# A parallel retention layer and a snake MLP on one core: two waits of the matrix engine's queue given other neighbours

## The chip, the cores and the metric

The kernel runs on one NeuronCore of a Trainium2 chip. A core has five engines with instruction queues of their own, each in program order: TensorE (PE, matrix products into PSUM), VectorE (DVE), ScalarE (ACT), GpSimd (POOL) and SyncE (SP, which here only issues transfers). They meet through semaphores. Data move between HBM and the on-chip memory SBUF by DMA, issued from SP's, POOL's or ACT's queue. The metric is the device time of one execution in microseconds (us); lower is better.

## The reference

Eight batches of 576 tokens with 8 heads of 64 go through a retention layer (attention without softmax, with a decay per head), and its output through a two-layer MLP:

```python
scores = scale * q @ k.T                    # per batch and head
ret = scores * Dmat                         # gamma[h] ** (i - j) for j <= i, else 0
x = (ret @ v) laid out as [4608, 512]       # tokens x (heads * 64)
h = x @ w_in                                # 512 -> 2048
g = h + sin(alpha * h) ** 2 / (alpha + 1e-9)
out = g @ w_out                             # 2048 -> 512, float32
```

## The kernel before, in words

**Attention.** The first 512 tokens of a batch are four chunks of 128, taken as two halves `p` of 256. q and k come in as float32 (`raw`, six buffers) by SP's queue and are cast to float16 with the decay factors (`cast_half`, L215 on VectorE or GpSimd, L210 on ScalarE). v, w_in and w_out come by GpSimd's queue. kT and qT are made by PE transposes into PSUM (`transposes`, L275) and a copy out (`take`, L236 and L237), or, for the second half of batch 2 and for all later batches, by DMA transposes (`crossed`, L232). `scores_pe` (L376) makes the products of kT and qT in two calls `y` per half; `scores_out` (L386) casts a result to SBUF on ScalarE as `scf`; `scores_mask` (L393) multiplies by the causal mask on VectorE into `ret`, from `scf` or straight from PSUM. `outer` (L312) makes k'v of a half or of both, `first_sum`, `faded`, `next_sum`, `to_state` and `chain` (L319 to L359) carry the states along; `values` (L462) and `states` (L488) add up the output, and `take_x` (L236, L237) writes it to `x`. The 64 last tokens of all batches are gathered into an eighth extra block.

**The MLP.** Block `n` is the 512 tokens of batch `n`. Its first product is made in 16 units of four matmuls (`gemm1_pe`, L584, into one of three PSUM banks "hp"), each followed by a sine (L593) and a square (L602) on ScalarE and a product on VectorE (L609) into `gT`. The second product of a block comes in 16 parts, four for each output chunk `c` of 128 tokens, each of four matmuls (`gemm2_pe`, L623); part `g` needs group `g` of w_out. A chunk adds up in one bank ("op", of which there is one, or "hp"), is copied to `osb` and written out.

**PSUM.** Eight banks: two double banks "mm" (transposes, scores, k'v, attention output take turns), three "hp", one "op".

**What sets the order.** The program is recorded in the written order, and each engine runs its own instructions in that order. Up to the start of block 2, the order is a table (`TABLE`, L637 on) of one step per line, read by `follow` (L1146). Its words here: `G2 n c g bank` four products of the second MLP layer; `SP`, `SO`, `SM` scores, their cast out, their mask (batch, half, y); `C b nm p t e` the cast of half of one tile on engine V, A or G; `WO g` the load of w_out's group g on GpSimd's queue; `TR` and `TK` PE transposes and their copies out; `OU` outer products. From block 2 on (L1160), a loop over the 16 units of block `n` puts, in each unit: the first product and its sine, then the steps that `at_unit` has set for this unit, then four products of the second layer of the block before (`next_second`) with the square and product around them. In block 2 the set steps are the attention of batch 3 (L1169 to L1172). The same loop casts batch 4 on GpSimd in units 5 to 9 (`CASTS`, L1159), issues its DMA transposes in units 7 and 10, and loads batch 5 from unit 12 on. The `chain` of batch 3 comes ahead of these casts on GpSimd.

Two parts of the second layer of block 1 are made inside the table, so in block 2 an output chunk closes in units 1, 5, 9 and 13, and there the order is: products, chunk copy (L633), square, product.

Of the kernel before, what the change touches and what calls it, by code (L numbers as in the profile page):

```python
# [16 lines left out]
def kernel(  # L17
# [103 lines left out]
    def load_v(b, p):  # L121
        t_ = work.tile([P, H, 2, D], F16, tag="v16", bufs=6, name="v16")
        half[b, "v", p] = t_
        if split(b):
            for g, s, xs in pieces(b, p):
                nc.gpsimd.dma_start(t_[halves(g), :, s], v[b, :, xs, :].rearrange("h i d -> i h d"))  # L126
            return None
        i_ = nc.gpsimd.dma_start(
            t_.rearrange("p h r d -> p h (r d)"),
            v[b, :, 256 * p : 256 * p + 256, :].rearrange("h (i r) d -> i h (r d)", r=2),  # L130
        )
        half[b, "v", p] = t_
        return i_

    def load_rest_v(G):
        t_ = work.tile([P, 2 * H, D], F16, tag="vr16", bufs=1, name="v16")
        for e in range(2):
            b = 4 * G + 2 * e
            nc.gpsimd.dma_start(t_[halves(e)], v[b : b + 2, :, 512:576, :].rearrange("b h i d -> i (b h) d"))
        half[G, "v", "rest"] = t_  # L140

    def load(b, nm, p):
        t_ = work.tile([P, H, 2 * D], F32, tag="raw", bufs=6, name=nm + "32")
        raw[b, nm, p] = t_
        if split(b) and nm == "k":
            for g, s, xs in pieces(b, p):
                nc.sync.dma_start(
                    t_[halves(g), :, 64 * s : 64 * s + 64], src[nm][b, :, xs, :].rearrange("h i d -> i h d")
                )
            return None  # L150
        return nc.sync.dma_start(t_, src[nm][b, :, 256 * p : 256 * p + 256, :].rearrange("h (i r) d -> i h (r d)", r=2))
# [13 lines left out]
    def load_rest(G, nm):  # L165
        t_ = work.tile([P, H, 2 * D], F32, tag="raw", bufs=6, name=nm + "32")
        for e in range(2):
            b = 4 * G + 2 * e
            nc.sync.dma_start(
                t_[halves(e)].rearrange("p h (x d) -> p (h x) d", d=D),  # L170
                src[nm][b : b + 2, :, 512:576, :].rearrange("b h i d -> i (b h) d"),
            )
        raw[G, nm, "rest"] = t_
# [29 lines left out]
    def cast_half(b, nm, p, t, eng):  # L203
        if (b, nm, p) not in half:
            half[b, nm, p] = work.tile([P, 4, 2, 2, D], F16, tag=nm + "16", bufs=nbuf[nm], name=nm + "16")
        if eng is nc.scalar:
            for y in range(4):
                for r in range(2):
                    h = head_of(y, t)
                    eng.mul(  # L210
                        half[b, nm, p][:, y, r, t, :], raw[b, nm, p][:, h, D * r : D * r + D],
                        fac[nm][:, 2 * h + r : 2 * h + r + 1],
                    )
            return
        eng.tensor_tensor(  # L215
            half[b, nm, p][:, :, :, t, :],
            raw[b, nm, p].rearrange("p (a t) (r d) -> p a t r d", t=2, r=2)[:, :, t],
            (ct if nm == "k" and split(b) else fac[nm]).rearrange("p (a t r) -> p a t r", a=4, t=2)[:, :, t].unsqueeze(3).to_broadcast([P, 4, 2, D]),
            MULT,
        )  # L220
# [354 lines left out]
    def gemm1(n, fc, o=None):  # L575
        gemm1_pe(n, fc, o)
        sine(n, fc)
# [20 lines left out]
    def square(n, fc, eng):  # L598
        hps, s_t = hps_of[n, fc]
        ss_t = work.tile([P, 512], F16, tag="ss", bufs=4, name="ss_t")  # L600
        if eng is nc.scalar:
            nc.scalar.activation(ss_t, s_t, mybir.ActivationFunctionType.Square)  # L602
        else:
            eng.tensor_tensor(ss_t, s_t, s_t, MULT)  # L604
        hps_of[n, fc] = hps, ss_t

    def product(n, fc):
        hps, ss_t = hps_of.pop((n, fc))
        nc.vector.scalar_tensor_tensor(gT[n][:, fc, :], ss_t, inva[:, fc : fc + 1], hps, MULT, ADD)  # L609
# [187 lines left out]
LK 2 q 1 w_in1  # L797
C 1 k 1 1 V
TK 1 0 q V
G2 0 3 1 hp  # L800
SP 1 0 1
SP 1 0 0
SO 1 0 1
C 1 k 1 0 V
SO 1 0 0
SM 1 0 0
C 1 q 1 1 G
WO 3
C 1 q 1 0 G
TR 1 1 q  # L810
TR 1 1 k
TK 1 1 q V
G2 0 2 1 hp
TK 1 1 k A
SP 1 1 0
# [169 lines left out]
    with tc.manual_schedule():  # L985
# [34 lines left out]
        def of(b):  # L1020
            if b not in att:
                att[b] = Attention(b)
            return att[b]
# [77 lines left out]
        def next_second(k=0):  # L1101
            n, u = second.pop(0)
            gemm2(n, u, "hp" if n == NBLK - 1 and u > 3 else "op")
# [56 lines left out]
        for n in range(2, NBLK):  # L1160
            A = A2
            todo = {}

            def at_unit(u, *fs):
                todo.setdefault(u, []).extend(fs)

            if A:
                if n == 2:
                    at_unit(1, lambda: A.scores(0, 0), lambda: A.scores(0, 1))  # L1169
                    at_unit(4, lambda: A.outer((0, 1)), lambda: A.chain((0, 1, 2, 3)), lambda: A.scores(1, 0))  # L1170
                    at_unit(7, lambda: A.scores(1, 1), lambda: A.values(0), lambda: A.add_states(0))
                    at_unit(10, lambda: A.values(1), lambda: A.add_states(1))  # L1172
                else:
                    at_unit(0, lambda: A.near(0), lambda: A.masked(0))
                    at_unit(0, lambda: A.outer((0, 1)), lambda: A.chain((0, 1, 2, 3)))
                    at_unit(4, lambda: A.near(1), A.late, lambda: A.masked(1))
                    at_unit(5, lambda: A.masked("late"))
                    if n == 5:
                        at_unit(8, lambda: A.all_values(0), rest[0].scores, lambda: A.add_states(0))
                        at_unit(11, lambda: A.all_values(1), rest[0].values, lambda: A.states(1, last=True))  # L1180
                        at_unit(11, lambda: A.take_x(1, V))
                    else:
                        at_unit(8, lambda: A.all_values(0), lambda: A.all_values(1))
                        at_unit(8, lambda: A.states(0, last=True), lambda: A.states(1, last=True))
                        at_unit(8, lambda: A.take_x(0, A_), lambda: A.take_x(1, V))
            bn = n + 2
            if bn < B:
                A2 = of(bn)
                at_unit(0, lambda: load_v(bn, 0), lambda: load_v(bn, 1))
                for i, u in enumerate(CASTS[n]):  # L1190
                    p, nm, t = i // 4, "kq"[i // 2 % 2], i % 2
                    at_unit(u, lambda p=p, nm=nm, t=t: cast_half(bn, nm, p, t, V if n > 2 else G_))
                at_unit(CASTS[n][3] + 1, lambda: A2.crossed(0))
                at_unit(CASTS[n][7] + 1, lambda: A2.crossed(1))
            else:
                A2 = None
            if bn + 1 < B:
                for i, (p, nm) in enumerate(HALVES):
                    at_unit(i + 12, lambda nm=nm, p=p: load(bn + 1, nm, p))
            if n in (3, 5):  # L1200
                at_unit(15, *[lambda nm=nm: load_rest((n - 3) // 2, nm) for nm in "kq"])
                at_unit(15, lambda: load_rest_v((n - 3) // 2))
            R = rest[(n - 4) // 2] if n in (4, 6) else None
            if n in (4, 6):
                at_unit(11 if n == 4 else 5, lambda: cast((n - 4) // 2, "k", "rest", V))
                at_unit(13 if n == 4 else 8, lambda: cast((n - 4) // 2, "q", "rest", V), lambda: R.crossed())
            if n == 7:
                at_unit(0, lambda: rest[1].scores())
                at_unit(2, lambda: rest[1].values())
            for u in range(16):  # L1210
                gemm1(n, u)
                for f in todo.get(u, []):
                    f()
                last = second[0][1] % 4 == 3
                if not last:
                    square(n, u, A_)
                    product(n, u)
                next_second()
                if last:
                    square(n, u, A_)  # L1220
                    product(n, u)
# [44 lines left out]
```

## Time and profile before

| | us |
|---|---|
| runs, median of 3 (lowest to highest) | 310.55 (310.01 to 310.61) |
| profiled execution | 309.65 |
| its span, first to last instruction | 307.6 |
| PE busy in the span | 296.1 |
| ScalarE busy | 227.0 |
| VectorE busy | 192.5 |
| GpSimd busy | 134.3 |

The profile is of one execution, and its times count from the span's first instruction. Matmuls are pipelined, so neighbouring ones overlap in the record; lengths of groups are therefore read from start to start. A timeline row gives start, length, engine, line, operation, output and inputs, the count, and in square brackets the idle time just before and what ended it. The views that the text names are the busy time by stretches, the waits by engine, the timelines by engine, the chain of work that ended last, and the transfers with their time from issue to landing. In the table's stretch (to about 77 us) the engines take turns in setting the pace; block 2 begins at 77.2 us.

### The profile page before, as it was taken

What the parts mean: (1) busy time and instruction counts of PE and PEld (TensorE: products, weight loads), DVE (VectorE), ACT (ScalarE), POOL (GpSimd) and SP (SyncE); (2) the same over time, 40 slices, a digit from 0 to 9 for tenths busy, and PEclk for the clock granted to TensorE, in tenths of its full rate; (3) what the DMA queues carried; (4) which work ended last, traced back from release to release, by engine and by line L of the source; (5) the groups of instructions that cost most, each with busy time, mean ns of one, the idle gap of its engine ahead of it and who ended that gap; (6) DMA issues with size and microseconds to landing.
All of it is one profiled execution on the core that took longest, in us unless ns stands there. A gap on an engine that the chain in (4) does not pass through costs nothing.

```text
span 307.6 us, 7628 instructions
## 1 busy us (share of the span) xinstructions
PE 296.1 (96%) x3134; PEld 152.6 (50%) x3134; DVE 192.5 (63%) x266; ACT 227.0 (74%) x378; POOL 134.3 (44%) x158
## 2 busy tenths in 40 slices
PE   7799989999899999999999999999999999999994
PEld 7475445544445444544454445544544444444444
DVE  3879848799554357956997699546665343444301
ACT  1579864899588887788778878787877888888810
POOL 3886744869969629702970297209000000000000
PEclk9999999999999999999999999999999999999998
DMA  8999999997999896999899979985331111122133
GB/s 216 220 206 230 238 195 279 191 248 119 165 187 216 170 212 139 145 174 228 177 156 189 186 189 187 152 127 87 70 68 37 35 34 36 34 54 49 35 68 68
DMA packets 118018, 44.74 MB, mean 145 GB/s; under 512 B 84433, under 2 KB 113505, under 8 KB 117985
## 3 DMA queue, kind: packets, MB, share of 16 engines
q1 hardware_dynamic: 83792, 35.08, 57.0%
q0 software_dynamic: 33600, 8.92, 31.1%
q8 instruction: 24, 0.39, 0.6%
q10 hardware_dynamic: 592, 0.28, 0.4%
q14 instruction: 10, 0.07, 0.1%
HBM read 36.91 MB, written 9.44 MB: 151 GB/s over the span
## 4 chain that ended last, share of the span: by engine, by line
PE 81%; DVE 10%; DMA 4%; POOL 1%; ACT 1%; issue 1%; SPq 0%; DVEq 0%; POOLq 0%
PE ops L623 37%; PE hps L584 32%; DVE ret L393 4%; DVE gT L609 2%; DMA qT<-q 2%; PE o L462 2%; PE o L488 2%; DMA q<-in_q_dram 2%; PE kv L312 1%; PE tr L275 1%; PE ops L1228 1%; PE sc L376 1%; PE sc L407 1%; PE hps L1067 1%; DVE kvs L334 1%
## 5 line engine op out<-in xcount | busy, mean ns | idle before, releaser
L609 DVE SCALAR_TENSOR_TENSOR gT<-ss_t,inva,hps 128x512 f16<-128x512 f16 x136 | 100.5, 744 | 79.9 <-ACT ss_t L602 79.4
L623 PE MATMUL ops<-w_out,gT 128*128 128x512 f16 x560 | 140.8, 379 | 0.0
L584 PE MATMUL hps<-x,w_in 128*128 128x512 f16 x480 | 120.9, 379 | 1.1 <-DVE gT L609 0.9
L593 ACT ACTIVATE s_t<-hps,alpha_t 128x512 f16<-128x512 f32 x136 | 92.8, 685 | 33.3 <-PE hps L584 32.3
L584 PEld LDWEIGHTS <-w_in 128*128 128x128 f16 x544 | 53.0, 98 | 64.5 <-issue 1.5
L623 PEld LDWEIGHTS <-gT 128*128 128x128 f16 x560 | 53.0, 98 | 60.9 <-DVE gT L609 0.3
L602 ACT ACTIVATE ss_t<-s_t 128x512 f16<-128x512 f16 x127 | 79.9, 631 | 2.6
L346 POOL TENSOR_TENSOR s<-kvs,cn 128x512 f16<-128x512 f32 x28 | 30.6, 1092 | 58.4 <-ACT kvs L319 50.5
L633 ACT COPY osb<-ops 128x512 f32<-128x512 f32 x31 | 18.1, 585 | 13.5 <-PE ops L623 13.3
L126 POOL DMA_DIRECT2D v<-in_v_dram x32 | 22.0, 730 | 0.0
L393 DVE TENSOR_TENSOR ret<-sc,mask 128x1024 f16<-128x1024 f32 x12 | 14.4, 1214 | 5.7 <-PE sc L376 5.7
L215 DVE TENSOR_TENSOR q<-q,cn 128x512 f16<-128x512 f32 x17 | 15.2, 920 | 3.9 <-DMA q<-in_q_dram 3.8
L584 PE MATMUL hps<-x_rest,w_in 128*128 128x512 f16 x64 | 16.4, 379 | 0.0
L215 POOL TENSOR_TENSOR q<-q,cn 128x512 f16<-128x512 f32 x14 | 14.8, 1069 | 0.4 <-DMA q<-in_q_dram 0.4
L432 DVE TENSOR_TENSOR ret<-sc,two 128x1024 f16<-128x1024 f32 x12 | 14.6, 1217 | 0.0
L236 ACT CAST x<-o 128x1024 f16<-128x1024 f32 (+1 forms) x13 | 10.8, 851 | 4.0 <-PE o L488 3.4
L604 POOL TENSOR_TENSOR ss_t<-s_t 128x512 f16<-128x512 f16 x10 | 10.4, 1057 | 6.3 <-ACT s_t L593 3.7
L359 POOL TENSOR_TENSOR kvs<-s,kvs 128x256 f32<-128x256 f32 x15 | 11.5, 769 | 1.2
L358 POOL TENSOR_TENSOR s<-kvs,cn 128x256 f32<-128x256 f32 x15 | 10.9, 730 | 0.0
L462 PE MATMUL o<-ret,v 64*64 64x128 f16 (+1 forms) x512 | 9.7, 213 | 1.1 <-DVE ret L393 1.0
L462 PEld LDWEIGHTS <-v 64*64 64x64 f16 x512 | 7.5, 107 | 5.6 <-issue 4.2
L215 POOL TENSOR_TENSOR k<-k,cn 128x512 f16<-128x512 f32 x9 | 9.9, 1115 | 0.0
(74 smaller groups left out, 210.7 us busy)
## 6 DMA issues: line engine op xcount, KB each, us to landing
out_dram<-osb SPq DMA_DIRECT2D x70, 128.0 KB, 2.9
q<-in_q_dram SPq DMA_DIRECT2D x14, 512.0 KB, 7.1
k<-in_k_dram SPq DMA_DIRECT2D x32, 128.0 KB, 4.6
k<-in_k_dram SPq DMA_DIRECT2D x7, 512.0 KB, 7.4
q<-in_q_dram SPq DMA_DIRECT2D x8, 256.0 KB, 5.1
v<-in_v_dram POOLq DMA_DIRECT2D x8, 256.0 KB, 5.7
w_in<-in_moe_w_in_dram POOLq DMA_DIRECT2D x4, 512.0 KB, 7.5
w_out<-in_moe_w_out_dram POOLq DMA_DIRECT2D x4, 512.0 KB, 7.9
```

Source lines behind the costliest of these rows:

```text
L126: nc.gpsimd.dma_start(t_[halves(g), :, s], v[b, :, xs, :].rearrange("h i d -> i h d"))
L215: eng.tensor_tensor(half[b, nm, p][:, :, :, t, :], raw[b, nm, p].rearrange("p (a t) (r d) -> p a t r d", t=2, r=2)[:, :, t], (ct if nm == ...
L346: (eng or nc.gpsimd).tensor_tensor(d_, self.kvs[:, n].unsqueeze(2).to_broadcast([P, 4, 2, D]), g2.unsqueeze(3).to_broadcast([P, 4, 2, D]), ...
L393: nc.vector.tensor_tensor(ret.rearrange("p t (z x) -> p (t z) x", z=2)[:, :, 0:n], sc.rearrange("p t (z x) -> p (t z) x", z=2)[:, :, 0:n], ...
L432: nc.vector.tensor_tensor(ret.rearrange("p t (a x) -> p (t a) x", a=n), sc.rearrange("p t (a x) -> p (t a) x", a=n), m_.unsqueeze(1).to_br ...
L462: nc.tensor.matmul(o[g][halves(t), x0 : x0 + 128].rearrange("p (r i) -> p r i", r=2)[:, :, i0:], x, y, start=(t, g) not in begun, stop=las ...
L584: nc.tensor.matmul(hps, w_in16[:, a, fc * P : (fc + 1) * P], x_of[n][:, a], start=(a == 0), stop=(a == KT - 1),)
L593: nc.scalar.activation(s_t, hps, mybir.ActivationFunctionType.Sin, bias=0.0, scale=alpha_t[:, fc : fc + 1],)
L602: nc.scalar.activation(ss_t, s_t, mybir.ActivationFunctionType.Square)
L609: nc.vector.scalar_tensor_tensor(gT[n][:, fc, :], ss_t, inva[:, fc : fc + 1], hps, MULT, ADD)
L623: nc.tensor.matmul(ops[n, c], gT[n][:, fk, c * P : (c + 1) * P], w_out16[:, fk, :], start=(fk == 0), stop=(fk == FC - 1),)
L633: nc.scalar.copy(osb, ops.pop((n, c)))
```

## The change

Two places. In the table, for batch 1: the four products `G2 0 3 1` go from ahead of the first half's scores to behind them; the mask `SM 1 0 0` goes from ahead of the second half's transposes to behind the copy of their qT; the load `WO 3` goes from between GpSimd's two casts of q to behind both. In block 2, each of the four groups of set steps for batch 3 comes one unit later. Nothing is added or taken out.

```diff
 TK 1 0 q V
-G2 0 3 1 hp
 SP 1 0 1
 SP 1 0 0
+G2 0 3 1 hp
 SO 1 0 1
 C 1 k 1 0 V
 SO 1 0 0
-SM 1 0 0
 C 1 q 1 1 G
+C 1 q 1 0 G
 WO 3
-C 1 q 1 0 G
 TR 1 1 q
 TR 1 1 k
 TK 1 1 q V
+SM 1 0 0
 G2 0 2 1 hp
 TK 1 1 k A
 SP 1 1 0
```

```diff
                 if n == 2:
-                    at_unit(1, lambda: A.scores(0, 0), lambda: A.scores(0, 1))
-                    at_unit(4, lambda: A.outer((0, 1)), lambda: A.chain((0, 1, 2, 3)), lambda: A.scores(1, 0))
-                    at_unit(7, lambda: A.scores(1, 1), lambda: A.values(0), lambda: A.add_states(0))
-                    at_unit(10, lambda: A.values(1), lambda: A.add_states(1))
+                    at_unit(2, lambda: A.scores(0, 0), lambda: A.scores(0, 1))
+                    at_unit(5, lambda: A.outer((0, 1)), lambda: A.chain((0, 1, 2, 3)), lambda: A.scores(1, 0))
+                    at_unit(8, lambda: A.scores(1, 1), lambda: A.values(0), lambda: A.add_states(0))
+                    at_unit(11, lambda: A.values(1), lambda: A.add_states(1))
```

## The prediction

> **What bounds the kernel now.** The row of busy time by stretches comes first: before and after 81.3 us, the end of the last wait that the matrix engine has.
>
> ```profile
> 81.30:291.00 209.70, 209.70 (x2042) 101.31 (x2032) 129.31 (x164) 166.91 (x263) 76.01 (x93) 1.00 0.84 127
> 28.00:81.30 53.30, 50.02 (x655) 25.73 (x653) 41.77 (x64) 40.85 (x78) 38.18 (x41) 1.00 1.12 211
> ```
>
> Columns: stretch, length, then busy time of PE, its weight loads, DVE, ACT, POOL, the granted clock, DMA. From 81.3 to 291 PE is busy 209.70 of 209.70 us at clock 1.00: whatever moves its work earlier there moves the end, and whatever makes it wait is paid in full. From 28 to 81.3 it idles 53.30 - 50.02 = 3.28 us. The waits of PE, the view read next, name three of these where the change is: 0.9 us for ACT's scf, 0.3 for VectorE's qT, 0.8 for qT from a DMA; the rows below carry each in brackets. Then the timelines of PE, ACT, DVE and POOL around 40 us (start, length):
>
> ```profile
> 38.02 1.89 PE L623 MATMUL ops<-w_out,gT 128*128 128x512 f16 x8
> 39.84 0.64 PE L376 MATMUL sc<-qT,kT 64*64 64x128 f16 x32
> 41.37 0.61 PE L275 MATMUL tr<-ident,q 128*128 128x128 f16 x8 [0.89 <-ACT scf L386]
> 41.81 0.61 PE L275 MATMUL tr<-ident,k 128*128 128x128 f16 x8
> 43.61 0.42 PE L376 MATMUL sc<-qT,kT 64*64 64x128 f16 x16 [0.33 <-DVE qT L237]
> ...
> 38.22 1.01 ACT L236 COPY kT<-tr 128x1024 f16<-128x1024 f16 x1 [0.32 <-PE tr L275]
> 40.30 1.93 ACT L386 CAST scf<-sc 128x1024 f16<-128x1024 f32 x2 [1.08 <-PE sc L376]
> 42.46 1.01 ACT L236 COPY kT<-tr 128x1024 f16<-128x1024 f16 x1 [0.23 <-PE tr L275]
> ...
> 38.86 0.93 DVE L215 TENSOR_TENSOR k<-k,cn 128x512 f16<-128x512 f32 x1
> 42.26 0.69 DVE L393 TENSOR_TENSOR ret<-scf,mask 128x1024 f16<-128x1024 f16 x1 [2.48 <-ACT scf L386]
> 42.87 0.68 DVE L237 COPY qT<-tr 128x1024 f16<-128x1024 f16 x1
> ...
> 37.92 1.31 POOL L215 TENSOR_TENSOR q<-q,cn 128x512 f16<-128x512 f32 x1
> 39.19 0.81 POOL L107 DMA_DIRECT2D w_out<-in_moe_w_out_dram  x1
> 40.02 1.06 POOL L215 TENSOR_TENSOR q<-q,cn 128x512 f16<-128x512 f32 x1
> ```
>
> Here ACT is the link: its score casts start only when the scores do, and those stand behind eight products. The transposes at 41.37 wait for the first cast and start 1.07 after it does (40.30); GpSimd's second cast of q, behind the issue of w_out's load, ends at 40.02 + 1.06 = 41.08, in time. VectorE's mask at 42.26, waiting for the second cast, holds up the copy of qT that the next scores need.
>
> **The front, step by step.** A hand-over costs about 0.05 us (qT's copy ends at 42.87 + 0.68 = 43.55, the scores start at 43.61). Four products take 0.86: eight matmuls of this size lie between 89.33 and 91.06 in the rows of block 2, 1.73 us (half the distance from 38.02 to the scores would be 0.91; I take the steady figure).
> - Four of the eight products go behind the scores. The first four then end their issue at 38.02 + 0.86 = 38.88, and the scores wait for kT: 38.22 + 1.01 + 0.05 = 39.28 instead of 39.84. So PE idles 0.40 there, and gains 0.56.
> - ACT's casts start 0.46 after the scores (40.30 - 39.84): 39.74; with the 1.07 and the 1.93 of the row, the transposes may start at 40.81 and both casts are done by 41.67. PE does its scores (0.64) and the four moved products (0.86) by 40.78. So the transposes start at 40.81, not 41.37: the products now fill the former wait, and the casts still set it.
> - GpSimd's second cast, ahead of w_out's issue, starts about 39.19 and takes between 1.06 (alone) and 1.31 (the row beside VectorE's work): it ends by 40.25 to 40.50. Neither end binds against 40.81; I take 1.31, since VectorE's 38.86 row overlaps it.
> - The Trainium skill, SBUF — State Buffer, "Who interferes with whom", speaks against this move: a VectorE instruction with two SBUF inputs and a GpSimd one that reads SBUF exclude each other, the first holding the port to its end. By that rule the cast would start after VectorE's 38.86 + 0.93 = 39.79 and end near 40.85, the transposes would start near 40.90, and the front would gain 0.56 instead of 0.65, an estimate of 309.15 us for the whole. The rows of 1.31 and 0.93 beside each other fit it; they do not prove it.
> - kT's copy starts 0.65 after the transposes of k begin (42.46 - 41.81). Those begin at 40.81 + 0.44 = 41.25, so the copy runs 41.90 to 42.91; ACT is free from 41.67. qT's copy no longer stands behind the mask: the transposes of q end at 40.81 + 0.61 = 41.42, the copy by about 42.15. The mask then runs in VectorE's free time, and its reader is far off (the value products at 47.8 in the row below).
> - The next scores start at 42.96 instead of 43.61, now held by kT instead of qT. **Gain of the front: 0.65 us**, with about 0.4 us of idle PE before the first scores and 0.4 before the next (42.96 less 41.25 + 0.44 + 0.86, when the transposes of k and the four products after them are issued) left over.
>
> Does 0.65 last? What could stay at its old clock time are transfers:
>
> ```profile
> w_out<-in_moe_w_out_dram POOLq DMA_DIRECT2D x1, 512.0 KB, 8.8
> 37.02 0.89 POOL L128 DMA_DIRECT2D v<-in_v_dram  x1
> DMA packets 568, 0.15 MB, mean 183 GB/s; under 512 B 566, under 2 KB 568, under 8 KB 568
> ...
> DMA packets 196, 0.20 MB, mean 201 GB/s; under 512 B 0, under 2 KB 196, under 8 KB 196
> ...
> 42.91 0.86 SPq L151 DMA_DIRECT2D k<-in_k_dram  x1
> k<-in_k_dram SPq DMA_DIRECT2D x1, 512.0 KB, 8.4
> ...
> 47.79 0.45 PE L462 MATMUL o<-ret,v 64*64 64x128 f16 x16
> 48.85 3.63 PE L623 MATMUL ops<-w_out,gT 128*128 128x512 f16 x16
> 52.41 0.95 PE L462 MATMUL o<-ret,v 64*64 64x128 f16 x32
> 52.81 1.28 DVE L215 TENSOR_TENSOR k<-k,cn 128x512 f16<-128x512 f32 x2
> ```
>
> The first two rows are the last load of w_out (39.19 + 8.8 = 47.99) and the v load issued on the same queue before it. The two packet rows are of 42.0 to 42.8 and 43.5 to 44.5: first small packets alone, then large ones alone. So GpSimd's queue is at the v load's packets until about 42.5, and w_out's, issued at 39.19, stand behind them. An issue about 1.06 to 1.3 later, at 40.25 to 40.50, still comes before that, so I take a landing unchanged at 47.99; the other end is 1.06 later, 49.05. The products that need it are the sixteen at 48.85, now 48.20: covered by 0.21. Keys of batch 2 land at 42.91 + 8.4 = 51.31, and VectorE wants them at 52.81 - 0.65 = 52.16: covered by 0.85.
>
> **Block 2.**
>
> ```profile
> 78.94 1.03 PE L584 MATMUL hps<-x,w_in 128*128 128x512 f16 x4
> 80.80 0.64 PE L376 MATMUL sc<-qT,kT 64*64 64x128 f16 x32 [0.84 <-DMA qT<-q]
> ...
> 73.97 1.80 SPq L232 DMA_TRANSPOSE qT<-q  x1
> qT<-q SPq DMA_TRANSPOSE x1, 6.7
> ```
>
> The transpose of qT lands at 73.97 + 6.7 = 80.67, PE is free 0.84 earlier. One unit later the scores come after unit 1's four products and unit 2's four matmuls: 78.94 + 3 x 0.86 = 81.52 without the front's gain, 80.87 with it. The landing, moved with the front, is 80.02; unmoved, 80.67. Either way it is there first. **Gain: 0.84 us**, whole, because PE had no other wait behind it.
>
> What the later slots meet (lengths and distances inside a unit are those of before):
>
> ```profile
> 86.66 0.71 PE L312 MATMUL kv<-v,k 64*64 64x64 f16 x64
> 87.59 1.04 PE L623 MATMUL ops<-w_out,gT 128*128 128x512 f16 x4
> 89.33 1.03 PE L623 MATMUL ops<-w_out,gT 128*128 128x512 f16 x4
> 91.06 1.03 PE L623 MATMUL ops<-w_out,gT 128*128 128x512 f16 x4
> ...
> 87.49 1.01 ACT L319 COPY kvs<-kv 128x1024 f32<-128x1024 f32 x1
> 90.39 0.58 ACT L633 COPY osb<-ops 128x512 f32<-128x512 f32 x1 [0.17 <-PE ops L623]
> ```
>
> Unit 5 closes an output chunk, so the copy of kv (1.01) now stands ahead of that chunk's copy (0.58) on ACT, and the single bank of the chunk must be empty when unit 6's products start. Counted from the outer products: kv's copy runs 0.83 to 1.84; the closing products start at 0.93, their copy 1.06 later (90.39 - 89.33), at 1.99 to 2.57; the bank is wanted 1.73 after 0.93, at 2.66. So it costs nothing, by 0.09; the other end is 0.92 (the 1.01 less this margin).
>
> The outer products themselves come at 86.66 + 1.73 - 1.49 = 86.90, 0.24 later by the clock, and GpSimd's chain and its casts of batch 4 with them:
>
> ```profile
> 101.15 1.37 SPq L232 DMA_TRANSPOSE qT<-q  x1
> qT<-q SPq DMA_TRANSPOSE x1, 3.2
> q<-in_q_dram SPq DMA_DIRECT2D x1, 512.0 KB, 10.3
> 110.67 0.42 PE L407 MATMUL sc<-qT,kT 64*64 64x128 f16 x16
> ```
>
> qT of batch 4 is issued at 101.39 and, at 3.2, lands at 104.6; block 3's first scores ask for it at 110.67 - 1.49 = 109.18. Covered by 4.6 us. The moved masks and copies of x keep three units or more to their readers, and a mask that stands ahead of a unit's product on VectorE did so in the unit before; these I cost at nothing, the distances inside a unit being the same.
>
> **The sum:** 0.65 + 0.84 = 1.49 us. The profiled execution took 309.65 us, its span 307.6 (2.05 around it); it becomes 308.16. The median of the runs is 310.55, 0.90 above the profiled one, so I forecast 310.55 - 1.49 = **309.06**.
>
> **Rivals.**
> 1. *The front's gain is given back to w_out's load.* If its landing moves with its issue, to 49.05, the sixteen products start at 49.09, 0.24 later than before, and the value products at 52.65. Before, the second half of those waited until about 52.9 for a mask, so about 0.1 to nothing of the 0.65 is left: 309.62 to 309.71. For: the cover is 0.21 only. Against: the packets' order.
> 2. *The copy of kv delays the chunk's copy in unit 5.* Up to 0.92 us lost: 309.06 + 0.92 = 309.98. For: a margin of 0.09. Against: both copies' times follow PE, which spaces them.
> 3. *The change doesn't do what it says:* both waits come back at full size at the next instruction: 310.55. For the front, kT could take over from qT entirely; against, kT's own chain starts at ACT's casts, which do move.
> 4. *Slower: the late transposes of batch 4.* GpSimd's chain leaves 109.18 - 101.39 = 7.79 us for qT. The trace has 3.2 here, 6.7 at 73.97, and 10.3 for the slowest load above. At 10.3 it lands at 111.69, PE waits 2.51, and the run ends 1.02 later than before, 311.6. It is slower from a landing time of 7.79 + 1.49 = 9.3 us on. For: transfers are the least steady thing in this trace. Against: more than twice its measured time.
>
> **Chances.** Forecast 0.60; rival 1 0.15; rival 2 0.07; rival 3 0.07; rival 4 0.11. A measurement of this kernel can tell about 0.2%, 0.62 us, from no change. Faster by more: the forecast and rival 1, 0.75; within: rivals 2 and 3, 0.14; slower: rival 4, 0.11. The range goes up to 310.1, past rival 2, leaving out rivals 3 and 4 (0.18). Down, the 0.90 us by which the runs exceed the profiled execution may lie in part in the two waits that go: all of it would give 308.16; I take 308.3.
>
> **What would show it.** Right: PE's waits for qT by DMA (0.84) and for scf (0.89) gone; scores near 39.3, transposes near 40.8 to 40.9, the next scores near 43.0 behind kT; the sixteen products near 48.2 without a wait; scores of block 2 near 80.9; PE busy without a break from there on. Wrong: PE waiting for w_out or k between 48 and 53, a wait of PE on ACT's osb near unit 6, or on qT at block 3's start; or the front's shift gone by 55 us.

## The result, and the profile after

| | before | changed |
|---|---|---|
| runs, median (lowest to highest), us | 310.08 (309.43 to 311.42), 9 runs | 308.99 (308.28 to 309.61), 9 runs |
| ratio to before, 95% interval | | 0.9956 (0.9940 to 0.9972) |
| profiled execution, its span, us | 309.65, 307.6 | 308.69, 306.7 |

The changed kernel is faster by 0.44%, about 1.4 us, with an interval from 0.9 to 1.9. (The two medians lie only 1.09 apart; the means of the same runs, 310.27 and 308.91, lie 1.36 apart.) The forecast, 309.06, started from the median of three runs, 310.55; six more runs bring that median to 310.08. So the forecast's difference of 1.49 is to be compared with these 1.4, and that 309.06 and 308.99 nearly meet is partly luck.

The busy time by stretches of the changed kernel (columns as in the prediction):

```profile
28.00:81.30 53.30, 51.34 (x634) 26.04 (x633) 42.14 (x65) 41.67 (x80) 39.35 (x41) 1.00 1.13 215
81.30:290.00 208.70, 208.70 (x2056) 100.97 (x2055) 129.30 (x164) 166.59 (x263) 75.89 (x93) 1.00 0.82 127
```

The second row is the prediction's premise once more: from 81.3 us on PE is busy in 208.70 of 208.70 us. In the first row PE's idle time is down from 3.28 to 53.30 - 51.34 = 1.96 us. Where it is left, PE's waits from 28 to 290 us (line, releaser: us in all, times, longest):

```profile
PE hps L584 <- DVE gT L609: 0.6, 2, 0.3
PE ops L623 <- DMA w_out<-in_moe_w_out_dram: 0.5, 1, 0.5
PE sc L376 <- ACT kT L236: 0.5, 2, 0.2
```

The waits for scf (0.89) and for qT from the DMA (0.84) are gone. In their place stand two of 0.24 for kT, at the two places of the forecast (which had about 0.4 at each), and one of 0.5 for w_out's load, which was a rival. PE's timeline, and behind the first "..." the rows of ACT, VectorE and GpSimd:

```profile
38.61 1.03 PE L623 MATMUL ops<-w_out,gT 128*128 128x512 f16 x4
39.87 0.64 PE L376 MATMUL sc<-qT,kT 64*64 64x128 f16 x32 [0.24 <-ACT kT L236]
40.45 1.04 PE L623 MATMUL ops<-w_out,gT 128*128 128x512 f16 x4
41.41 0.61 PE L275 MATMUL tr<-ident,q 128*128 128x128 f16 x8
43.56 0.42 PE L376 MATMUL sc<-qT,kT 64*64 64x128 f16 x16 [0.24 <-ACT kT L236]
49.34 3.61 PE L623 MATMUL ops<-w_out,gT 128*128 128x512 f16 x16 [0.50 <-DMA w_out<-in_moe_w_out_dram]
54.78 0.61 PE L275 MATMUL tr<-ident,k 128*128 128x128 f16 x8
81.65 0.64 PE L376 MATMUL sc<-qT,kT 64*64 64x128 f16 x32
90.18 1.03 PE L623 MATMUL ops<-w_out,gT 128*128 128x512 f16 x4
109.79 0.42 PE L407 MATMUL sc<-qT,kT 64*64 64x128 f16 x16
...
38.81 1.01 ACT L236 COPY kT<-tr 128x1024 f16<-128x1024 f16 x1 [0.32 <-PE tr L275]
89.52 0.59 ACT L633 COPY osb<-ops 128x512 f32<-128x512 f32 x1
...
37.85 1.02 DVE L215 TENSOR_TENSOR k<-k,cn 128x512 f16<-128x512 f32 x1 [0.64 <-DMA k<-in_k_dram]
42.50 0.69 DVE L237 COPY qT<-tr 128x1024 f16<-128x1024 f16 x1 [2.18 <-PE tr L275]
51.31 1.53 DVE L393 TENSOR_TENSOR ret<-scf,mask 128x1024 f16<-128x1024 f16 x1
...
38.65 2.57 POOL L215 TENSOR_TENSOR q<-q,cn 128x512 f16<-128x512 f32 x2
41.17 0.82 POOL L107 DMA_DIRECT2D w_out<-in_moe_w_out_dram  x1
```

This execution is 0.59 us late already at kT's copy (38.81, before 38.22), ahead of all that was changed. So the rows are read from that copy's start. The first scores come 1.06 behind it (before 1.62), the second half's 4.75 (before 5.39): 0.64 gained. The transposes of batch 2, at 54.78, come 15.97 behind it (before 16.39): 0.42 are left. Block 3's first scores, at 109.79, come 70.98 behind it (before 72.45): 1.47 gained, beside the 1.49 of the sum. From there to the span's end it is 196.9 to 197.1 us in every trace of this case.

### The profile page after: what moved, and what is told of

It reads as the page before. It is cut to its first block, busy times and chain, and to the rows that moved or that the text cites. A ratio compares the mean times of both kernels' runs of the same rounds, so it can differ in the third digit from the quotient of the medians.

```text
span 306.7 us, 7628 instructions
## 1 busy us (share of the span) xinstructions
PE 296.4 (97%) x3134; PEld 152.8 (50%) x3134; DVE 191.6 (62%) x266; ACT 227.0 (74%) x378; POOL 135.2 (44%) x158
## 4 chain that ended last, share of the span: by engine, by line
PE 79%; DMA 6%; DVE 5%; POOL 5%; ACT 2%; issue 2%; POOLq 0%; DVEq 0%; ACTq 0%
PE ops L623 36%; PE hps L584 33%; DMA w_in<-in_moe_w_in_dram 3%; DMA w_out<-in_moe_w_out_dram 3%; DVE gT L609 2%; PE o L462 2%; PE o L488 2%; PE hps L1067 2%; POOL v L128 1%; POOL q L215 1%; PE ops L1228 1%; DVE ret L393 1%; POOL ss_t L604 1%; ACT s_t L593 1%; PE kv L312 1%
## 5 line engine op out<-in xcount | busy, mean ns | idle before, releaser
L215 DVE TENSOR_TENSOR q<-q,cn 128x512 f16<-128x512 f32 x17 | 14.1, 854 | 4.3 <-DMA q<-in_q_dram 4.3
L215 POOL TENSOR_TENSOR q<-q,cn 128x512 f16<-128x512 f32 x14 | 15.5, 1120 | 0.1
L215 DVE TENSOR_TENSOR k<-k,ct 128x512 f16<-128x512 f32 x12 | 10.0, 830 | 0.0
```

What stands on the lines that cost most here:

```text
L215: eng.tensor_tensor(half[b, nm, p][:, :, :, t, :], raw[b, nm, p].rearrange("p (a t) (r d) -> p a t r d", t=2, r=2)[:, :, t], (ct if nm == ...
```

## The experiments

Theory at the start: both gains are real and independent; in the front the scores follow kT, in block 2 the landing of qT is passed. Rivals: one part does nothing, or w_out's load takes back part of the front. The table gathers what the traces say of all kernels, in us behind the start of kT's copy (for block 2: behind the transposes of batch 2, up to block 3's first scores). The last columns are medians and ratios to before on the same chip with 95% interval; e5, e6 and e7 have a single time each. Medians of different rows are not to be compared, since the runs were made on several chips, on which the median of before lies between 310.07 and 310.58.

| kernel | kT's copy at | first scores | second half's scores | transposes of batch 2 | block 2 | median, us | ratio |
|---|---|---|---|---|---|---|---|
| before | 38.22 | 1.62 | 5.39 | 16.39 | 56.06 | 310.08 | |
| changed | 38.81 | 1.06 | 4.75 | 15.97 | 55.01 | 308.99 | 0.9956 (0.9940–0.9972) |
| e3, changed, again | 39.38 | 1.44 | 5.12 | 16.12 | 55.05 | 309.59 | 0.9968 (0.9949–0.9988) |
| e13, changed, again | 38.79 | 1.56 | 5.24 | 16.24 | 55.18 | 308.94 | 0.9954 (0.9935–0.9973) |
| e1, table alone | 38.66 | 1.06 | 4.75 | 15.76 | 55.99 | 310.07 | 0.9996 (0.9975–1.0017) |
| e2, slots alone | 39.28 | 1.62 | 5.39 | 16.39 | 55.05 | 309.83 | 0.9978 (0.9957–0.9998) |
| e7, products back | 39.45 | 1.62 | 5.31 | 16.31 | 55.06 | 309.84 | |
| e5, mask back | 38.76 | 1.06 | 4.84 | 15.84 | 55.10 | 308.74 | |
| e6, w_out's load back | 38.52 | 1.63 | 5.32 | 16.32 | 55.19 | 309.03 | |
| e4, w_out's load early | 39.16 | 1.54 | 5.22 | 16.22 | 55.15 | 309.06 | 0.9965 (0.9940–0.9990) |
| e8, qT's copy first | 38.43 | 1.06 | 4.75 | 15.76 | 55.10 | 308.66 | 0.9951 (0.9935–0.9968) |
| e12, the same again | 40.10 | 1.07 | 4.75 | 15.77 | 55.13 | 309.05 | 0.9964 (0.9947–0.9980) |
| e9, e8 and e4 | 39.78 | 1.06 | 4.75 | 16.30 | 55.10 | 308.60 | 0.9957 (0.9938–0.9976) |
| e10, slots at 0, 3, 6, 9 | 38.91 | 1.53 | 5.21 | 16.22 | 57.03 | 311.22 | 1.0030 (1.0013–1.0046) |

### The two parts apart, and the whole again

e1 is the changed table with the old slots, e2 the old table with the new slots, e3 the changed kernel as it is. The only edit of e1 against the changed kernel:

```diff
-                    at_unit(2, lambda: A.scores(0, 0), lambda: A.scores(0, 1))
+                    at_unit(1, lambda: A.scores(0, 0), lambda: A.scores(0, 1))
...
-                    at_unit(11, lambda: A.values(1), lambda: A.add_states(1))
+                    at_unit(10, lambda: A.values(1), lambda: A.add_states(1))
```

e2's edit is the table's diff of the change, taken back.

> The table's three moves alone; block 2's slots as in the kernel before. My theory: two separate waits went, so the parts add. Counted from the first transposes of batch 1 (tr of q, first half), the second layer's products and transposes around 55 us come 0.5 to 0.65 us earlier than before; the matrix engine waits about 0.5 for w_out's last load; the wait for qT in block 2 stays at about 0.8 because the transposes by DMA move with the front. Time 0.5 to 0.65 us below before. Rival A, the front's gain is given back (to w_out's load, or because qT lands at its old time): the wait for qT grows to about 1.4 and the time equals before within 0.15 us.

> Block 2's slots one unit later alone; the table as before. My theory: the 0.84 us wait for qT goes whole, nothing appears in units 5 to 13 or at block 3's start, the front looks as before (transposes of the second half 4.82 us after those of the first half); time 0.8 to 0.9 us below before. Rival B, part is lost again to the copy of kv ahead of the chunk's copy in unit 5: a wait of the matrix engine on the copy osb near unit 6, and under 0.5 us gained. Rival C, all of the change's gain is in this part: this kernel equals the changed one within 0.2 us.

> The changed kernel once more, beside the others on one chip. The profile of the changed kernel reached the first transposes of batch 1 0.72 us later than that of before, in a stretch that the change does not touch. My theory: that is the scatter of the first loads between executions, so here the start differs again, by up to 0.7 either way, and the stretch from the first transposes to the end is again 1.5 to 1.6 us shorter than in before; time 1.1 to 1.5 us below before. Rival: the change itself delays the start (the same 0.7 us appears again here and in the table-only kernel).

The waits divide as expected, except that the table alone shows no wait for w_out's load, where 0.5 was expected. One wait of PE in the table alone, then the scores of block 2 with the slots alone:

```profile
PE sc L376 <- DMA qT<-q: 0.9, 1, 0.9
```

```profile
82.59 0.64 PE L376 MATMUL sc<-qT,kT 64*64 64x128 f16 x32
```

With the table alone the wait for the DMA's qT is whole (0.87): the landing came earlier along with the front, so the wait neither shrank nor grew. With the slots alone it is gone and block 2 is shorter by 1.01, while the front is that of before to the hundredth. The clock is coarser: 0.9996 for the table alone is no gain that can be measured, although its trace shows 0.63 of it (16.39 less 15.76), and its interval reaches to -0.8 us. So the size of the front's gain rests on traces, and only that of the slots (0.9978) on the clock as well, just.

e3 brought the first surprise. It is the same program as the changed kernel, and its front gains 0.27 in place of 0.64. From the first transposes of batch 1 to the end it is only 0.7 shorter than before, where 1.5 to 1.6 was expected. Part of this lies ahead of the edits: between those transposes and kT's copy pass 1.54 to 2.79 us in these traces, whatever the kernel. An expectation that counts from the transposes takes this in (e2's 4.82 came as 5.26 for it), so the table counts from kT's copy. The rest lies in the front itself. The rows of e13, a third execution of that program, show what happens (PE, then VectorE, ACT, GpSimd):

> The changed kernel a third time. My theory: from kT's copy to the second half's scores 4.75 us when VectorE's cast of k has its load by 0.8 us before kT's copy ends, and 5.1 to 5.25 us when it has not (5.39 in before); no wait for qT in block 2; time 0.9 to 1.4 us below before. Rival, that the start is later because of the change: from the span's start to the first transposes of batch 1 0.6 us more than before's 36.55 once more.

```profile
40.35 0.64 PE L376 MATMUL sc<-qT,kT 64*64 64x128 f16 x32 [0.73 <-DVE qT L237]
44.03 0.42 PE L376 MATMUL sc<-qT,kT 64*64 64x128 f16 x16 [0.24 <-ACT kT L236]
...
37.79 1.90 DVE L215 TENSOR_TENSOR k<-k,cn 128x512 f16<-128x512 f32 x1 [1.17 <-DMA k<-in_k_dram]
39.62 0.68 DVE L237 COPY qT<-tr 128x1024 f16<-128x1024 f16 x1
...
38.79 1.01 ACT L236 COPY kT<-tr 128x1024 f16<-128x1024 f16 x1 [0.32 <-PE tr L275]
...
38.06 2.53 POOL L215 TENSOR_TENSOR q<-q,cn 128x512 f16<-128x512 f32 x2
```

PE waits for qT, not for kT. kT is ready at 38.79 + 1.01 = 39.80, qT only at 39.62 + 0.68 = 40.30. VectorE's copy of qT stands behind its cast of the second half of k (`C 1 k 1 1 V`), and that cast took 1.90 us here and 1.02 in the first trace of the changed kernel. The expectation for e13 blamed a late load, and that failed: k's load was there at 37.79, 2.0 ahead of the end of kT's copy, and by its rule 4.75 should have come in place of 5.24. Counted from kT's copy the cast began 1.00 ahead of it, against 0.96 in the first trace of the changed kernel; what came late was the cast's end. e4, e6 and e10 are of the same kind (begun 0.96 to 0.99 ahead, 1.83 to 1.97 long); only in e3 was the load itself late as well (0.66 ahead, 1.44 long). In e2 the four products ahead of the scores covered this: its front is the old one although that cast took 1.85 in it.

### qT's copy ahead of the cast of k

New theory: the front's gain depends on the cast of k, because qT's copy is queued behind it; with the copy first, the scores follow kT every time. Rival: kT and qT are both late for some common reason, such as k's load, and the order on VectorE doesn't matter.

```diff
-C 1 k 1 1 V
 TK 1 0 q V
+C 1 k 1 1 V
 SP 1 0 1
```

> The changed kernel with the copy of the first half's qT put ahead of VectorE's cast of k's second half. In the second look at the changed kernel that cast waited for its load until 38.72 us, the copy of qT stood behind it until 40.76, and the scores began at 40.81 behind the copy; in the first look the load landed at 37.8 and kT set the scores. My theory: this is why the front's gain comes and goes, since the four moved products no longer cover the copy. So here the scores begin with kT's copy (about 0.05 after it), whenever the load lands, with no wait of the matrix engine for qT, and the transposes of the second half come 2.1 us after kT's copy begins plus at most 0.6; time 0 to 0.4 us below the changed kernel. Rival, the load itself sets the front (through the cast of k that the second half's transposes read): the transposes of the second half then wait for VectorE's k, and nothing is gained when the load is late.

> The version with the first qT's copy ahead of VectorE's cast of k, again, beside the changed kernel on one chip. My theory: the scores begin 1.06 us after kT's copy and the second half's scores 4.75 us after it, in every look; time 0 to 0.4 us below the changed kernel and 1.2 to 1.8 below before. Rival, its lower time so far is scatter: equal to the changed kernel within 0.1 us.

The rows of PE and VectorE in e12:

```profile
41.17 0.64 PE L376 MATMUL sc<-qT,kT 64*64 64x128 f16 x32 [0.24 <-ACT kT L236]
...
40.10 0.69 DVE L237 COPY qT<-tr 128x1024 f16<-128x1024 f16 x1 [2.85 <-PE tr L275]
40.71 1.28 DVE L215 TENSOR_TENSOR k<-k,cn 128x512 f16<-128x512 f32 x2
```

In both executions the scores come 1.06 and 1.07 behind kT's start, the second half's 4.75, and batch 2's transposes 15.76 and 15.77, although everything was 1.67 us later in e12 than in e8. e9 below, which has the same order, gives 1.06 and 4.75 once more. Nor did the loads come more kindly. In e8 k's load landed at 30.24 + 7.2 = 37.4 and GpSimd's cast of q began only 0.3 later (0.3 in e9 too), as in the traces whose cast of k was long; the two casts of k together took 1.89 in place of e12's 1.28, behind the copy, where PE did not wait for it:

```profile
30.24 2.00 SPq L151 DMA_DIRECT2D k<-in_k_dram  x1
k<-in_k_dram SPq DMA_DIRECT2D x1, 512.0 KB, 7.2
37.70 2.07 POOL L215 TENSOR_TENSOR q<-q,cn 128x512 f16<-128x512 f32 x2
39.04 1.89 DVE L215 TENSOR_TENSOR k<-k,cn 128x512 f16<-128x512 f32 x2
```

The rival falls, and the theory stands: the three traces of the changed kernel itself scatter from 15.97 to 16.24. By the clock the two versions can't be told apart (0.9951 and 0.9964 against 0.9956, 0.9968 and 0.9954).

### The table's moves one by one

Each of the three moves taken back alone, against the changed kernel:

```diff
+G2 0 3 1 hp
 SP 1 0 1
 SP 1 0 0
-G2 0 3 1 hp
```

```diff
 SO 1 0 0
+SM 1 0 0
...
 TK 1 1 q V
-SM 1 0 0
```

```diff
 C 1 q 1 1 G
-C 1 q 1 0 G
 WO 3
+C 1 q 1 0 G
```

> The changed kernel with the four products back ahead of the first half's scores. My theory: they carry the front's gain; the scores come about 1.6 us after kT's copy begins (1.62 in before, 1.06 in the changed kernel), ScalarE's casts and all behind them with it, and the second half's scores 5.3 us after kT's copy (5.39 in before, 4.75 in the changed kernel). Rival, the earlier casts of q and the mask's move make the gain: 4.75 to 4.9 us.

> The changed kernel with the mask back ahead of the copy of the second half's qT. My theory: that copy was not the only link, since kT's copy on ScalarE ends at nearly the same time; so the second half's scores come only about 0.1 us later (4.84 us after the first half's kT copy begins, instead of 4.75, with an early load). Rival, as the prediction's working has it, the mask's place is a part of its own: 0.3 us or more later.

> The changed kernel with w_out's last load back between GpSimd's two casts of q. My theory: the second cast then ends 0.4 us or more after ScalarE's first cast, so the second half's transposes wait for GpSimd instead of following the four products at once; the second half's scores come 4.9 to 5.0 us after the first half's kT copy begins when k's load is early (4.75 in the changed kernel), and 5.1 to 5.3 when it is late, where the first scores wait anyway. w_out's load is issued about 1.3 us earlier, and nothing waits for it. Rival, the load's place costs nothing in the front, because ScalarE's casts are the later of the two: 4.75.

With the products back, the transposes wait for ACT's scf as before, and almost nothing of the gain is left (second half's scores at 5.31, before 5.39):

```profile
42.60 0.61 PE L275 MATMUL tr<-ident,q 128*128 128x128 f16 x8 [0.89 <-ACT scf L386]
44.76 0.42 PE L376 MATMUL sc<-qT,kT 64*64 64x128 f16 x16 [0.24 <-ACT kT L236]
```

With the mask back, the first scores keep their 1.06 and the second half's come at 4.84 behind qT:

```profile
43.60 0.42 PE L376 MATMUL sc<-qT,kT 64*64 64x128 f16 x16 [0.33 <-DVE qT L237]
```

So the mask's move is worth 0.09, the difference between waiting for qT and for kT there, as the 0.08 left in e7 confirms; the products' move carries the rest. The trace with w_out's load back says nothing of that move: its cast of k was one of the long ones (1.97), its first scores came at 1.63, and a wait for qT of 0.81 covers whatever the load did. What that place is worth, and with it the earlier second cast of q on GpSimd, is open.

### The last load of w_out

In the changed kernel GpSimd issues the load at 41.17, or 40.58 in the clock of before, 1.39 later than the 39.19 there. The transfer row (KB, us from issue to landing):

```profile
w_out<-in_moe_w_out_dram POOLq DMA_DIRECT2D x1, 512.0 KB, 8.1
```

It lands at 49.3 and PE waits 0.50 for it. Theory: that wait costs what lies between 15.97 and 15.76, and an issue ahead of v's load takes it away. (From the second half's scores to batch 2's transposes 11.00 to 11.01 us pass in twelve of the fourteen traces, before included. The changed kernel's first trace has 11.22 and e9 has 11.55, and these are the two in which PE waits for w_out.) Rival: the load only trades places in the queue with another one that PE needs sooner.

```diff
 WO 2
+WO 3
...
-LV 2 0
...
-WO 3
+LV 2 0
 TR 1 1 q
```

> The changed kernel with w_out's last load issued right behind the one before it, in the place of a load of v for batch 2, and that load of v behind GpSimd's casts in its place. My theory: the 0.50 us wait for w_out is the late issue (41.17 in the changed kernel) showing through; issued about 37.8, the load lands by about 47 and the wait goes; of its 0.50 us only 0.15 to 0.3 comes back, because VectorE's mask (ending at 52.84) then holds the value products. The v load lands by about 50 and is wanted near 59.8, so nothing waits for it. Time 0.1 to 0.3 us below the changed kernel. Rival, the landing is set by the traffic of all queues and not by the issue: the load lands after 48.5 all the same, and the wait and the time stay within 0.1.

> Both further moves on top of the change: the copy of qT ahead of the cast of k, and w_out's last load ahead of the load of v. My theory: no wait of the matrix engine for w_out and none for the first qT; from the first transposes of batch 1 to block 3's first scores 72.3 us or less (74.12 in before, 72.52 in the changed kernel's first profile, 73.39 in its second); time 0.3 to 0.7 us below the changed kernel and 1.3 to 1.9 below before. Rival, the loads of batch 1 and 2 set the front: 73 us or more, and the time of the changed kernel within 0.2.

In e4 the last load, issued at 37.7, lands at 47.2 and no product waits for it; but its front is held by a cast of k of 1.84, so e9, with qT's copy first, is the clean case. PE's row and the issues and landing of the two loads in e9:

```profile
45.71 1.89 PE L623 MATMUL ops<-w_out,gT 128*128 128x512 f16 x8 [0.51 <-DMA w_out<-in_moe_w_out_dram]
```

```profile
37.48 1.56 POOL L107 DMA_DIRECT2D w_out<-in_moe_w_out_dram  x2
```

```profile
w_out<-in_moe_w_out_dram POOLq DMA_DIRECT2D x1, 512.0 KB, 8.2
```

The third load, issued at 37.48, now lands 8.2 later at 45.7, and PE waits 0.51 for that one, at 45.71. The wait has moved to an earlier load, and batch 2's transposes come at 16.30, later than with e8's order alone (15.76). So the further gain that was expected of the two moves together did not come: from the first transposes of batch 1 to block 3's first scores it is 73.4, where 72.3 or less was expected. That the two loads traded places, as the rival says, is not shown: the third load took 7.1 in e4, in the same order, and up to 7.8 (e10) with v's load behind it. The wait of the changed kernel itself is no fixed cost either: nine traces issue the last load from behind both casts, and eight of them have no wait for it (landings in e3, e13 and e8 at 48.6, 47.4 and 47.7).

### The slots two units earlier

This asks whether the wait in block 2 is the landing of qT less the schedule, as the prediction's working has it: two units earlier than the changed slots, the wait should come back and be longer than before.

```diff
-                    at_unit(2, lambda: A.scores(0, 0), lambda: A.scores(0, 1))
+                    at_unit(0, lambda: A.scores(0, 0), lambda: A.scores(0, 1))
...
-                    at_unit(11, lambda: A.values(1), lambda: A.add_states(1))
+                    at_unit(9, lambda: A.values(1), lambda: A.add_states(1))
```

> The changed kernel with block 2's four groups in units 0, 3, 6 and 9, two units earlier than the change and one earlier than before. My theory: qT's landing alone sets the first scores, so the matrix engine stands at them for 0.84 + 1.73 = about 2.6 us, all of it paid: 2.6 us above the changed kernel and 1.1 to 1.7 above before. Rival, the wait is only a shift of work that the other engines make good in it: under 1 us above the changed kernel.

PE's rows, and the time to landing of that transpose:

```profile
79.83 0.64 PE L376 MATMUL sc<-qT,kT 64*64 64x128 f16 x32 [1.18 <-DMA qT<-q]
86.40 0.71 PE L312 MATMUL kv<-v,k 64*64 64x64 f16 x64 [0.64 <-DMA v<-in_v_dram]
```

```profile
qT<-q SPq DMA_TRANSPOSE x1, 5.5
```

The wait is back, and block 2 takes 57.03, 1.9 more than the 55.01 to 55.18 of the new slots, of which 1.18 + 0.64 = 1.82 are these two rows; the time, 311.22, is the only one above before (1.0030). Kind and place are as expected, the size is not. The transpose took 5.5 us here and not 6.7, and its issue came 0.3 earlier behind batch 2's transposes (19.04 against 19.36), which makes its wait smaller; and a second wait showed, for v of batch 3 at the outer products, which the expectation did not have.

## Why the prediction was right, and which steps were not

**The forecast's sum.** 1.49 was forecast; the first trace gives 1.47 from kT's copy to block 3, the runs 1.4 (0.9 to 1.9). That the trace is so close is in part luck. Two deviations cancel in it: w_out's wait took about 0.2 from the front, and the stage behind the front came out 0.2 shorter than the wait that went (55.01 against 56.06 is 1.05, for a wait of 0.84). The trace of before has there a third wait of a first product for gT, 0.36 at 72.55, that the changed one has not; why it went is not shown. And the trace is one in which the front gave its 0.64: the same program gave 1.28 in e3 and 1.03 in e13.

**The step that failed: "the scores wait for kT".** It held in the first trace (1.06 behind kT's start, as computed), in e1, and in e5. In e3, e13, e4, e6 and e10, five of the eight traces with the products behind the scores and qT's copy in its old place, PE waited 0.6 to 0.8 us for qT, and the gain at the second half's scores was 0.07 to 0.27. The prediction took the copies of before as given. VectorE's rows of before at this place:

```profile
37.20 1.14 DVE L215 TENSOR_TENSOR k<-k,cn 128x512 f16<-128x512 f32 x1 [0.71 <-DMA k<-in_k_dram]
38.25 0.68 DVE L237 COPY qT<-tr 128x1024 f16<-128x1024 f16 x1
```

qT's copy is queued right behind the cast of k's other half. Here it ended at 38.25 + 0.68 = 38.93, only 0.35 ahead of the 39.28 that the forecast took for the scores, and in the five traces that cast was 0.3 to 0.8 us longer than the 1.14 here (in e3 its load was late too). Four products had covered it; their move took the cover away. The working priced the idle time that the move makes, but not what it uncovers: the other operand of the scores, with the queue in front of it. e8, e12 and e9 show that this order is the cause; what makes the cast long is treated in the last section and stays open.

**Products, mask and the chain by ACT.** Right where kT leads: transposes at 41.41 - 0.59 = 40.82, forecast 40.81; the second half's scores at 42.97, forecast 42.96. One detail was wrong without effect: qT's second copy does not start when the transposes of q are done (41.46 by the forecast) but together with kT's, at 42.50 - 0.59 = 41.91, after a wait of 2.18 for `tr`.

**GpSimd's second cast.** Forecast to end at 40.50 by rows, and near 40.85 by the Trainium skill's rule; it ended at 38.65 + 2.57 - 0.59 = 40.63, between the two. It does not bind: the transposes start at 40.82 without a wait, and the products fill PE until then.

**Rival 1, w_out's load.** Half of it came. The load was issued later than forecast (40.58 against at most 40.50) and landed at 49.3 - 0.6 = 48.7, between the forecast ends 47.99 and 49.05. PE waited 0.50, but only about 0.2 of it reached the transposes of batch 2 (15.97, against 15.76 in the e1 and e8 traces without the wait), because the value products wait for VectorE's mask without it too. The rival left that mask at its old time of about 52.9; it moved with the front and ended at 51.31 + 1.53 - 0.59 = 52.25. The price of 0.56 to 0.65 was therefore too high, and the wait itself came in one of nine traces with the load issued there.

**Block 2.** Right. The scores at 81.65 are 81.06 by the clock of before, 0.2 later than the 80.87 forecast, as much as the front brought less at 54.78, and no transfer holds them up. Rival 2 is out: the chunk's copy ends at 89.52 + 0.59 = 90.11, the products that want the bank start at 90.18 without a wait. The margin is 0.07; forecast was 0.09. Rival 4 is out: the transpose of qT for batch 4, issued at 102.18, took 3.1 us and was there 4.5 us before block 3's scores at 109.79 (forecast 4.6). It was not provoked by an experiment. Rival 3 is out by the waits.

**The runs' level.** The forecast let the 0.90 between median and profiled execution lie partly in the waits. The traces speak against this, though before has only one: e2's waits in the front are those of before, and the large scatter lies ahead of the change. The kT copy of batch 1 starts anywhere from 38.22 to 40.10, and between the same program's three traces from 38.79 to 39.38. It follows k's first load of that batch. In before, and by the last two rows in e12:

```profile
24.63 0.58 SPq L151 DMA_DIRECT2D k<-in_k_dram  x1
k<-in_k_dram SPq DMA_DIRECT2D x1, 512.0 KB, 9.3
33.96 3.93 ACT L210 ACTIVATE k<-k,cn 128x64 f16<-128x64 f32 x16 [0.23 <-DMA k<-in_k_dram]
...
26.39 0.58 SPq L151 DMA_DIRECT2D k<-in_k_dram  x1
k<-in_k_dram SPq DMA_DIRECT2D x1, 512.0 KB, 9.4
```

The load lands at 24.63 + 9.3 = 33.9 and at 26.39 + 9.4 = 35.8; ACT's casts and PE's transposes follow, and kT's copy starts 4.3 later in both, and 4.3 to 4.4 later in all fourteen traces. The rival of e3 and e13, that the later start in the changed kernel's trace was the change's doing, falls with this: the first transposes of batch 1 stand at 37.27 there, 36.68 in e13 (the same program), 37.17 in e2 (the old table) and 36.55 before.

## What to carry to other kernels

When work is moved from ahead of a wait to behind it, list everything that this work had been covering, every operand of the waiting instruction with its own queue, and not only the wait it is moved away from. A copy that a busy engine waits for should not stand behind a cast whose length or load varies: exchanging the two lines showed no cost here and made the front's scores repeat to 0.01 us in three executions. One trace of a kernel is one sample of its transfers: margins under half a microsecond against a load or a cast came out on either side from one execution to the next.

## What the runs showed of the hardware that was not expected

VectorE's cast of k (two SBUF inputs, 128x512) took 1.01 to 1.14 us in the five traces where its record starts 0.5 to 0.8 us ahead of GpSimd's first cast of q, and 1.83 to 1.97 in the five where it starts only 0.2 to 0.35 ahead; in e3 it starts 0.19 behind and took 1.44. The row of before above is of the first kind (37.20, with GpSimd's cast at 37.92 in the prediction's rows); the rows of VectorE and GpSimd in e6 are of the second:

```profile
37.53 1.97 DVE L215 TENSOR_TENSOR k<-k,cn 128x512 f16<-128x512 f32 x1 [1.09 <-DMA k<-in_k_dram]
...
37.87 1.07 POOL L215 TENSOR_TENSOR q<-q,cn 128x512 f16<-128x512 f32 x1
```

In e6 GpSimd's cast ends at 38.94 after an ordinary 1.07, and VectorE's ends at 39.50, 0.56 later, or about the 0.64 that one of two such casts takes in e12 (1.28 for two). It reads as if VectorE's work began only when GpSimd's had ended. The Trainium skill, SBUF — State Buffer, "Who interferes with whom", has such an exclusion of a VectorE instruction with two SBUF inputs and a GpSimd one that reads SBUF. The length of 1.97 agrees with that; that the instruction which issues first keeps the port does not show in these records, as VectorE's began 0.34 earlier and was the one held up. This was seen over the traces and not set up by an experiment; why 0.2 to 0.35 of a lead is not enough, and why even the shorter kind takes 0.4 to 0.5 more than those 0.64, stays open.

A DMA transpose of one 128x1024 tile took 6.8 us to landing at 73.75 in the changed kernel (6.6 to 7.1 in the eleven other traces that show its landing, e10 aside), 5.5 in e10 for the same tile, and 3.1 at 102.18 (3.0 to 3.3 over all traces). So its size alone does not set its time; that the traffic around it does is likely and was not tried. The 5.5 is most of what the expected size missed in e10.
